# Expanding probabilities by masked products in a recurrent-memory attention kernel, with the output halves exchanged and the instruction order written anew

## The chip, the cores and the metric

The kernel runs on one core of a Trainium2 chip. The metric is the device time of one execution in microseconds, median of several runs. One more execution is recorded by the hardware profiler; its durations are what the text works with.

## The reference

Four blocks follow each other on a sequence of 2048 tokens of width 512: A, B, A, B, each with a residual sum and a layer norm in front.

```
# A: recurrent memory, 64 segments of 32 tokens, 8 memory rows, 32 heads of 128
for s in range(64):
    h = concat([mem, x[32*s : 32*s+32]])          # 40 rows
    q, k, v = h @ Wq, h @ Wk, h @ Wv              # 32 heads
    p = softmax(mask(q @ k.T * scale))            # tokens causal, memory rows see all
    o = (p @ v) @ Wo                              # 40 x 512
    mem = o[:8]                                   # the next segment's memory
    outs.append(o[8:])
# B: linear attention, 32 heads of 16
pq, pk = phi(q), phi(k)                           # phi(t) = where(t > 0, t + 1, exp(t)) + 1e-6
o = (pq @ (pk.T @ v)) / (pq @ sum(pk) + 1e-6) @ wo
```

The memory of segment s + 1 needs the finished output of segment s, so block A is a recurrence of 64 steps. The memory rows need only the memory queries; the outputs of the tokens feed nothing but the residual.

## The kernel before

**Tiling.** Every 128 x 128 weight block is used as four column tiles of 32, so that a matmul is issued four times, on the tiles (0, 32j). A step s handles one segment. Groups of four steps share 128 tokens (a "block" G with g = s mod 4). The last 8 tokens of each segment are handled together for the whole group ("left" rows).

**A step of block A** (`a_layer`, loop at L2446) issues, under names that the order table uses too:
- `kq0`, `kq1`, `v`: projections of the 40 rows by Wk, Wq, Wv (`project`, L2121 and, for matmuls that reuse loaded weights, L2010), each 512 columns wide, with copies out of PSUM by `evac` (L1893 on ScalarE, L1894 on VectorE, whichever the table names) and 32 x 32 transposes on VectorE (L2139).
- `mem0`, `mem1`: scores, softmax and weighted values of the 8 memory queries (`mem_attention`).
- `out`: 64 matmuls with Wo (`out_proj`, L2346). Their result lies in PSUM in two halves of 64 partitions that have to be added: one half is copied to `outW_sb` (`evac`), then the other half in PSUM and the copy are added into `y_sb` (L2355, on VectorE). An "urgent" output is that of a step; a non-urgent one is that of the left rows of a group.
- `next`: two sets of matmuls that turn the first 8 rows of y_sb round (L2372), and a copy into the input of the next step. `out` to `next` to `kq0` of step s + 1 is the recurrence.
- `res`: the output rows are moved by DMA into dx_sb, one on the POOL queue and one on SP's (L1909), and added to x (L2416).
- `x`: the attention of the 32 token queries (`x_attention`, L2262 on), whose result is used by `out` of step s + 1. The masked exponentials PQ (L2276) are summed (L2287), the reciprocal comes as exp(-ln) (L2290, L2292), the probabilities are normalised in place (L2294, and L2295 for the left keys). Then they are **expanded**: the partitions 32j to 32j + 31 hold the keys of head group j, and the matmuls need, for each j, a tile Pbx that is zero outside these partitions. Pbx is set to zero once, and each step makes four copies of 32 partitions x 256 elements, on ScalarE or VectorE. Pbl for the left keys is made by a masked product (L2301). The matmuls `pvx` (L2022) read Pbx, and their result is copied out.

**Block B** is interleaved. `b_in` handles 128 tokens: `layernorm` (L2058 to L2064), a transpose of the normalised rows by DMA from SP's queue (`turn`, L2049, kind "dtb"), projections (L2513), phi (L2486 to L2488) and sums. `prepare` normalises the next 128 tokens of block A and has them transposed in the same way (kind "dtx"), with five copies into the inputs of the steps. `b_out` has the queries transposed (kind "dtq").

**Order.** Nothing is scheduled on the chip: each engine runs its instructions in the order written, with semaphore waits. The order comes from the table PLACE, one entry for each (layer, step, name): a due time in ns for each operation in the order of its issue, with "a" (ScalarE) or "v" (VectorE) behind it where either engine could do it. `schedule` sorts all operations by these due times and gives out the eight PSUM banks in that order. The table was made by a planner that knew a cost for each operation; the numbers `cost` and `lat`, and the marks `quad` (start quadrant of what is read, and of what is written) are for that planner, and change nothing in the program itself.

Of the kernel before, what the change touches and what calls it, by code (L numbers as in the profile page):

```python
# [6 lines left out]
F32 = mybir.dt.float32  # L7
F32R = mybir.dt.float32r
ACTF = mybir.ActivationFunctionType
ALU = mybir.AluOpType  # L10
# [6 lines left out]
    (0, -9, 'setup'): '6123 501 3261 6844 6847 6850 7372 7373 7741 8707 11389 26847 27280 27283 30185 31770 36506 38205 39802 41695 45140 47037 6849 0 1070 1630 2700 3260 6121 6122 6124 6845 6846 6848 7371 7740 8300 10031 11387 11388 11536 12012 12013 12220 12780 13340 14071 14460 15020 15580 16140 36507 31771 16700 17260 17820 18373 27282a 7740 7966v 121034 26200 27281 29822 31769 33223 26849 27279 33872',  # L17
    (0, -4, 'start'): '8706v',
    (0, -2, 'left0'): '25336 25767 26846 27278 27918a 29821 30547v 31270',
    (0, -2, 'left1'): '29823 30186 30547 31271 32259a 32389 33224a 33509',  # L20
    (0, -2, 'leftv'): '35270 35702 36508 36665 37305a 37946 38425 38424a 39333 42302',
    (0, -2, 'prep'): '6120 6843 7037 7370 7742 8300 13340v 11386a 8533v 32390a 10032a',
    (0, -2, 'spin4'): '18429',
    (0, 0, 'kq0'): '24904 26415 27926 28573 29214v 32260 29214a 30184',
    (0, 0, 'kq1'): '14070 15020 15020 17260 26199 27918 28357 29005 18374v 26848 31270a 32752',
    (0, 0, 'mem0'): '31768 32752 35702 33509 36665 38092 40257 42302 43407 43810',
    (0, 0, 'mem1'): '34007 36133 36505 36665 36774 39801 39803 43409 44930 45625',
    (0, 0, 'next'): '48918 48972 49238v',
    (0, 0, 'out'): '44931 44932 45137 45347 46599 46818 47370 47588 48015a 48443',
    (0, 0, 'ql'): '31155v 33222v',  # L30
    (0, 0, 'v'): '40256 40258 41217 41219 42665v 41719a',
    (0, 0, 'x'): '37798 37954 38917 39332 39800 44674 43408a 40255v 40259a 40576v 44929 45138 47036 47095 48443 53855v 59925a 44674 44929 45566 46056 52710v 47038v',
    (0, 0, 'xl'): '500',
    (0, 1, 'kq0'): '50187 50188 50343 50775 52071v 53366 51639a 52502',
    (0, 1, 'kq1'): '51206 51638 51854 52285 51422 52070 52501 52717 52709a 53955 53856a 54093',
    (0, 1, 'mem0'): '53796 53854 54226 54819 54495 54876 55196 55952 55951 56442',
    (0, 1, 'mem1'): '54818 55196 55368 55953 55637 56114 56441 57401 56578 57403',
    (0, 1, 'next'): '59604 59658 59924v',
    (0, 1, 'out'): '56745 56964 57182 57400 57619 57839 58294 58295 58714a 59128',
    (0, 1, 'ql'): '50186v 37797a',  # L40
    (0, 1, 'res'): '66853 69592',
    (0, 1, 'v'): '52933 53365 53954 54496 55369v 55954a',
    (0, 1, 'x'): '56065 56440 57402 57619 57838 58853 58713v 58433v 58293v 58573v 59713 59414 59532 59770 59941 60357v 61029v 59355 59473 59712 59926 63405a 60150v',
    (0, 2, 'kq0'): '60165 60597 61028 61460 62756v 63619 63403a 63404',
    (0, 2, 'kq1'): '61892 62323 62539 62971 62107 62755 63187 63402 63677a 64680 63827v 64798',
    (0, 2, 'left0'): '32789 33221 38204 38917 40575a 41216 41694v 43407',
    (0, 2, 'left1'): '31826 32258 37097 41696 44067v 45136 45626a 47588',
    (0, 2, 'leftv'): '41218 45139 45624 46168 47588v 49345 49823 51206a 51206 51854',
    (0, 2, 'mem0'): '63618 64108 64679 64480 65161 65712 66473 66854 66845 67481',
    (0, 2, 'mem1'): '65503 65711 66204 66496 66472 66852 67171 67480 66963 67842',  # L50
    (0, 2, 'next'): '70334 70388 70654v',
    (0, 2, 'out'): '67694 67696 68577 69032 69033 69034 69593 69594 69595a 69962',
    (0, 2, 'prep'): '10030 10753 10947 11280 11535 12011 14073a 14074a 15580a 31272a 14072a',
    (0, 2, 'ql'): '56745v 60030v',
    (0, 2, 'res'): '70443 80542',
    (0, 2, 'v'): '63676 64208 64798 65071 65711a 66205v',
    (0, 2, 'x'): '66844 67480 67693 68108 68576 69591 69311v 69031v 69171v 69451v 70388 69726 69961 70442 70654 70973v 72191a 69785 69843 69902 70654 70972a 75960a',
    (0, 3, 'kq0'): '70972 71327 71758 72190 73054a 73919 73918v 73920',
    (0, 3, 'kq1'): '73053 73701 73917 74133 72622 72838 73323 73485 74839a 75762 74349a 75271',
    (0, 3, 'mem0'): '74348 75270 75642 75761 75961 76601 76711 77376 77376 77746',  # L60
    (0, 3, 'mem1'): '75370 75962 76602 76600 77208 77746 77869 78178 77746 78539',
    (0, 3, 'next'): '81000 81054 81319a',
    (0, 3, 'out'): '78178 78391 78807 79730 79731 80010 80012 80150 80425a 80543',
    (0, 3, 'ql'): '69731v 66907a',
    (0, 3, 'res'): '84592 87832',
    (0, 3, 'v'): '74407 74838 75428 75963 76600v 77209a',
    (0, 3, 'x'): '77415 77869 78390 78806 79274 79729 79869v 80009v 80149v 80149a 80288 80424 80541 80659 80888 84159v 84594a 80482 80600 80718 80776 81569v 82433v',
    (0, 4, 'kq0'): '81568 82000 82432 82863 84591a 85081 84160a 84595',
    (0, 4, 'kq1'): '83511 84374 84590 84806 83295 83727 83943 84158 85230a 85871 84806a 85302',
    (0, 4, 'mem0'): '85022 85302 86049 86048 86539 87288 87833 88902 88736 89139',  # L70
    (0, 4, 'mem1'): '86480 86538 87289 87288 88051 88268 88588 89252 89546 89885',
    (0, 4, 'next'): '92400 92454 93084a',
    (0, 4, 'out'): '90143 90483 90484 90485 90486 90963 90964 91625 91723a 92212',
    (0, 4, 'ql'): '80011a 79869a',
    (0, 4, 'res'): '95561 95991 85080 85871 86638 87831 88050 88518 88899 89140 89545v 90482 95345 91624 95985 95986 93833 90966 91626 92284 96274',
    (0, 4, 'v'): '85871 86048 86856 87400 88381a 88900v',
    (0, 4, 'x'): '87288 88380 89139 89465 90142 91624 91721a 90822v 90965a 91722v 91628 92152 92211 92270 93562 95344v 102252a 93563 93564 96854 98366 100384v 103118a',
    (0, 4, 'xl'): '2130',
    (0, 5, 'kq0'): '93565 93566 93832 94264 95562a 95984 95560v 95992',
    (0, 5, 'kq1'): '94695 94911 95127 95559 95343 95987 95990 96274 95983a 98481 96630a 97935',  # L80
    (0, 5, 'mem0'): '96913 96971 98366 97934 98480 98574 99186 99789 99791 99950',
    (0, 5, 'mem1'): '98477 98946 99066 99788 99790 99792 100073 100382 99950 101014',
    (0, 5, 'next'): '103383 103437 103702a',
    (0, 5, 'out'): '100383 101011 101012 101479 101480 101934 102074 102075 102427v 102777',
    (0, 5, 'ql'): '86050a 90962v',
    (0, 5, 'res'): '111729 109466',
    (0, 5, 'v'): '96630 97452 97502 97934 99187v 98574a',
    (0, 5, 'x'): '99793 100382 100594 101010 101478 101933 102073v 102637v 102425a 102076a 103480 103702 103703 103726 104819 106011a 107306v 103491 103702 103785 103844 105795v 107522v',
    (0, 6, 'bi'): '96914 97452 98367 98479 98482 98946 98478 102426 103119 109837 111575 112302 112818 115257 116071v 122296 125666 125780 128352 114679 115050 116913 129770',
    (0, 6, 'kq0'): '103956 104387 104931 105362 106658v 107730 106013a 107953',  # L90
    (0, 6, 'kq1'): '106657 106873 107089 107305 105794 106010 106226 106441 107729a 108975 107523a 108443',
    (0, 6, 'left0'): '55370 55519 58853 59128 62755v 73324 73701a 75960',
    (0, 6, 'left1'): '66204 66474 69596 81108 81747a 84593 86638a 88901',
    (0, 6, 'leftv'): '76603 80151 91627 91720 92454v 93083 93567 93561a 103117 106014',
    (0, 6, 'mem0'): '108384 108442 108976 109614 109465 110224 110916 110955 110357 111317',
    (0, 6, 'mem1'): '109405 109464 110223 109836 110600 110804 111727 111730 110915 111981',
    (0, 6, 'next'): '114624 114678 114944v',
    (0, 6, 'out'): '111726 111981 112162 112381 112599 112817 113036 113254 113714a 114142',
    (0, 6, 'prep'): '18373 24904 38092 41220 45755 53954 55368v 73322a 62971a 67695v 82000v',
    (0, 6, 'ql'): '101013v 104931v',  # L100
# [1672 lines left out]
def _build_kernel(nc, A_x, A_mem0, A_Wq, A_Wk, A_Wv, A_Wo, A_seg_len, B_wqkv, B_wo, out):  # L1773
# [274 lines left out]
    def turn(o, i, reads, writes, kind, lat=2.8):  # L2048
        add("sp", lambda e: e.dma_start_transpose(o, i), 1.2, reads=reads, writes=writes, dsem=kind, lat=lat)  # L2049
# [673 lines left out]
```

## Time and profile before

| | |
|---|---|
| median of 3 runs | 1614.55 us (1612.61 to 1621.16) |
| profiled execution | 1630.0 us |
| its span, first to last instruction | 1627.4 us |
| granted TensorE clock | 0.998 |
| TensorE busy | 1534.2 us (94%) |
| VectorE busy | 1226.8 us (75%) |
| ScalarE busy | 1059.4 us (65%) |
| GpSimd busy | 191.6 us (12%) |
| quadrant copies on ScalarE | 228, 94.3 us |
| quadrant copies on VectorE | 284, 62.2 us |

PE is TensorE's matmul row, PEld its weight loads, DVE is VectorE, ACT is ScalarE, POOL is GpSimd and SP is SyncE, which issues DMAs only. A line such as "PE pb L2372 <- DVE y_sb L2355" says that PE, at line 2372, sat idle until VectorE's instruction of line 2355 was done. A busy share is an average over the span. PE's ends are modelled, so that a busy PE need not be at its peak.

### The profile page before, as it was taken

How to read it: one execution, taken by the hardware profiler on the slowest of the kernel's cores; microseconds unless marked ns; L12 is line 12 of the kernel's file. 1: busy time of each engine (PE TensorE's matmuls, PEld its weight loads, DVE VectorE, ACT ScalarE, POOL GpSimd, SP SyncE). 2: the span in 40 equal slices, each digit the busy share in tenths (PEclk: the TensorE clock that was granted, in tenths of full speed). 3: DMA queues.
4: the chain of work that ended last, by engine and by line, in shares of the span. 5: the costliest groups of instructions: out<-in, count | busy, mean ns of one | idle time of the engine just before them, and what ended most of it. 6: DMA issues, size and time to landing. Idle time of an engine off the chain costs nothing.

```text
span 1627.4 us, 97760 instructions
## 1 busy us (share of the span) xinstructions
PE 1534.2 (94%) x48853; PEld 810.1 (50%) x40499; DVE 1226.8 (75%) x3601; ACT 1059.4 (65%) x3099; POOL 191.6 (12%) x388
## 2 busy tenths in 40 slices
PE   5889999999999999999899999999999999999997
PEld 1445555455555555555444555455555445555453
DVE  3778778877777877777678777777777777777777
ACT  2566666666666667666466677766677667676665
POOL 2011110111111011111101110111110111110110
PEclk9999999999999999999999999999999999999999
DMA  9310000110000001001101101111001110100115
GB/s 382 88 32 23 20 13 22 19 27 20 23 20 14 22 23 23 20 16 24 22 14 19 26 14 25 27 26 23 21 19 23 26 25 19 27 17 21 27 33 145
DMA packets 79348, 58.14 MB, mean 36 GB/s; under 512 B 58872, under 2 KB 73624, under 8 KB 77400
## 3 DMA queue, kind: packets, MB, share of 16 engines
q1 hardware_dynamic: 65912, 36.30, 8.5%
q0 software_dynamic: 12864, 15.46, 3.4%
q8 instruction: 350, 5.73, 1.5%
q14 instruction: 62, 0.51, 0.1%
q10 hardware_dynamic: 160, 0.14, 0.0%
HBM read 25.57 MB, written 10.35 MB: 22 GB/s over the span
## 4 chain that ended last, share of the span: by engine, by line
PE 68%; DVE 13%; DMA 10%; ACT 7%; issue 2%; POOL 0%; SPq 0%; DVEq 0%
PE pb L2121 25%; PE pb L2010 17%; PE pb L2346 12%; PE pb L2022 8%; DMA arena_sb<-arena_sb 5%; DVE arena_sb L1894 3%; ACT arena_sb L1893 2%; DMA dx_sb<-y_sb 2%; DMA Wv_sb<-in_A_Wv_dram 2%; DVE arena_sb L2139 2%; PE pb L2513 2%; PE pb L2210 1%; DVE y_sb L2355 1%; DVE arena_sb L2294 1%; PE pb L2372 1%
## 5 line engine op out<-in xcount | busy, mean ns | idle before, releaser
L1893 ACT ACTIVATE arena_sb<-pb 128x512 bf16<-128x512 f32 (+4 forms) x1032 | 499.6, 511 | 293.1 <-PE pb L2010 131.5
L1894 DVE CAST arena_sb<-pb 128x512 bf16<-128x512 f32 (+3 forms) x614 | 322.3, 533 | 105.7 <-PE pb L2010 64.9
L2121 PE MATMUL pb<-Wk_sb,arena_sb 128*32 128x512 bf16 x4096 | 363.3, 381 | 8.2 <-DMA Wk_sb<-in_A_Wk_dram 4.3
L2346 PE MATMUL pb<-Wo_sb,arena_sb 128*32 128x256 bf16 x10368 | 340.0, 273 | 5.7 <-issue 3.3
L2139 DVE STREAM_TRANSPOSE arena_sb<-arena_sb 128x256 f32<-128x256 f32 x640 | 263.3, 431 | 55.0 <-ACT arena_sb L1893 49.0
L2346 PEld LDWEIGHTS pb<-Wo_sb,arena_sb 128*32 128x32 bf16 x10368 | 257.7, 96 | 53.5 <-issue 15.9
L2022 PE MATMUL pb<-arena_sb 128*32 128x128 bf16 (+2 forms) x10800 | 266.6, 209 | 18.3 <-DVE arena_sb L1894 10.0
L2121 PE MATMUL pb<-Wq_sb,arena_sb 128*32 128x512 bf16 x3072 | 266.9, 379 | 3.3 <-DVE arena_sb L1894 2.8
L1909 POOL DMA_DIRECT2D dx_sb<-y_sb x252 | 128.4, 513 | 1198.5 <-DVE y_sb L2355 776.5
L2022 PEld LDWEIGHTS pb<-arena_sb 128*32 128x32 bf16 x10800 | 183.5, 96 | 149.5 <-DVE arena_sb L1894 45.5
L2121 PE MATMUL pb<-Wv_sb,arena_sb 128*32 128x512 bf16 x2560 | 251.4, 378 | 2.3 <-ACT arena_sb L1893 1.2
L2010 PE MATMUL pb<-Wv_sb,arena_sb 128*32 128x512 bf16 x2560 | 251.2, 378 | 0.0
L2121 PEld LDWEIGHTS pb<-Wk_sb,arena_sb 128*32 128x32 bf16 x4096 | 110.5, 97 | 196.4 <-issue 97.3
L2010 PE MATMUL pb<-Wq_sb,arena_sb 128*32 128x512 bf16 x2048 | 200.7, 379 | 0.0
L1893 ACT ACTIVATE arena_sb<-arena_sb 32x256 bf16<-32x256 bf16 (+2 forms) x411 | 146.9, 361 | 38.8 <-DVE arena_sb L2294 29.1
L2121 PEld LDWEIGHTS pb<-Wq_sb,arena_sb 128*32 128x32 bf16 x3072 | 83.8, 96 | 93.6 <-issue 43.6
L1894 DVE COPY arena_sb<-arena_sb 32x256 bf16<-32x256 bf16 (+2 forms) x502 | 100.8, 203 | 20.6 <-DMA arena_sb<-arena_sb 11.3
L2355 DVE TENSOR_TENSOR y_sb<-pb,outW_sb 64x256 bf16<-64x256 f32 x162 | 67.8, 419 | 55.4 <-ACT outW_sb L1893 51.3
L2258 DVE TENSOR_TENSOR arena_sb<-pb,arena_sb 128x128 bf16<-128x128 f32 x252 | 73.1, 290 | 47.3 <-PE pb L2022 15.2
L2121 PEld LDWEIGHTS pb<-Wv_sb,arena_sb 128*32 128x32 bf16 x2560 | 70.1, 95 | 66.1 <-issue 36.9
L2010 PE MATMUL pb<-Wk_sb,arena_sb 128*32 128x512 bf16 x1024 | 101.6, 379 | 0.0
L1893 ACT ACTIVATE outW_sb<-pb 64x256 f32<-64x256 f32 x130 | 49.0, 377 | 73.5 <-PE pb L2346 71.3
(110 smaller groups left out, 1793.2 us busy)
## 6 DMA issues: line engine op xcount, KB each, us to landing
Wk_sb<-in_A_Wk_dram SPq DMA_DIRECT2D x1, 4096.0 KB, 13.7
Wq_sb<-in_A_Wq_dram SPq DMA_DIRECT2D x1, 4096.0 KB, 24.1
Wv_sb<-in_A_Wv_dram SPq DMA_DIRECT2D x1, 4096.0 KB, 33.5
Wo_sb<-in_A_Wo_dram SPq DMA_DIRECT2D x16, 256.0 KB, 7.3
xs_scratch<-x_sb POOLq DMA_DIRECT2D x32, 128.0 KB, 2.2
pq_scratch<-arena_sb POOLq DMA_DIRECT2D x31, 128.0 KB, 2.4
x_sb<-xs_scratch POOLq DMA_DIRECT2D x16, 128.0 KB, 3.0
dx_sb<-y_sb SPq DMA_DIRECT2D x126, 12.0 KB
```

The source lines that it names most:

```text
L1893: return e.activation(o() if callable(o) else o, i() if callable(i) else i, ACTF.Copy)
L1894: return e.tensor_copy(o() if callable(o) else o, i() if callable(i) else i)
L1909: add(eng, lambda e: e.dma_start(o, i), 0.55 if eng == "pool" else 0.66, reads=reads, writes=writes, dsem="%s%d" % (kind, k), lat=lat + (0 ...
L2010: return pe.add_instruction(mybir.InstMatmult(name=nc.get_next_instruction_name(), engine=mybir.EngineType.PE, ins=[pe.lower_ap(x), pe.low ...
L2022: r = pe.matmul(o[q], w[:, q], x, start=start, stop=stop, skip_group_check=True, tile_position=(0, 32 * j))
L2121: r = pe.matmul(o, blk[:, c, :], w, start=(c == 0), stop=(c == 3), tile_position=(0, 32 * j))
L2139: add("dve", lambda v: v.transpose(dst, src(img[:, k, :].bitcast(F32))), 0.445, reads=[("img", k)], writes=[dkey])
L2210: r = pe.matmul(o, kT[:, hh, j // 2, :, j % 2], qT[:, hh, j // 2, :, j % 2].rearrange("p (k x) -> p k x", k=5), start=True, stop=True, til ...
L2258: add("dve", lambda v: v.tensor_tensor(oTb[:, s % NO, 16 * b:16 * b + 16, 0:8].rearrange("p (i j) q -> p j i q", i=4), heads(pv.f32()[:, 0 ...
L2346: r = pe.matmul(tl.f32()[32 * j:32 * j + 32, 0:256], oT[:, 4 * hh + n, :], Wo_sb[:, 8 * n + hh, 256 * d:256 * d + 256], start=(hh == 0 and ...
L2355: add("dve", lambda e: e.tensor_tensor(y_sb[0:64, k, :], tl.f32()[a, 0:256], outW[c, v, :], ALU.add), c_dve(256), reads=[("outW", w)], til ...
L2513: r = pe.matmul(dst.f32()[q, :], xlnT[:, c, q], wqkv_sb[:, c, o:o + D], start=c == 0, stop=c == 3, skip_group_check=True, tile_position=(0 ...
```

## The change

1. The four copies into quadrants of Pbx become two VectorE products, one for each half b of the heads, of the normalised probabilities with the block mask `bo_sb` (ones where the partition belongs to group j). Each product writes all 128 partitions, zeros included, so that Pbx need not be set to zero beforehand. The `pvx` matmuls of a half wait for that half's product alone.
2. In `out_proj` the two halves change places: for urgent outputs partitions 0 to 63 are copied and 64 to 127 read by the sum in PSUM, for non-urgent ones the other way round. `quad` tells the planner.
3. `turn` has a longer `lat` (3.6, and 4.4 for kind "dtb", in place of 2.8), and PLACE is written anew throughout, 1509 entries, with other due times and other choices of engine.

```diff
 PLACE = {
-    (0, -9, 'setup'): '6123 501 3261 6844 ...
+    (0, -9, 'setup'): '6124 561 6121 6125 ...
...
-    def turn(o, i, reads, writes, kind, lat=2.8):
-        add("sp", lambda e: e.dma_start_transpose(o, i), 1.2, reads=reads, writes=writes, dsem=kind, lat=lat)
+    def turn(o, i, reads, writes, kind, lat=3.6):
+        add("sp", lambda e: e.dma_start_transpose(o, i), 1.2, reads=reads, writes=writes, dsem=kind, lat=4.4 if kind == "dtb" else lat)
...
-            for j in range(4):
-                q = slice(32 * j, 32 * j + 32)
-                add(ANY, copy(Pbx[q, j, :, :], px[q]),
-                    {"act": c_act(256, 0, 1), "dve": c_dve(256, 4)}, quad=(j, j), reads=pk + [("Px", r2)], writes=[("Pbx", j)])
+            for b in range(2):
+                add("dve", lambda v, b=b: v.tensor_tensor(
+                    Pbx[:, :, b, :].rearrange("p j (k x) -> p j k x", k=4),
+                    px[:, b, :].rearrange("p (k x) -> p k x", k=4).unsqueeze(1).to_broadcast([128, 4, 4, 32]),
+                    bo_sb[:, :].rearrange("p (j x) -> p j x", j=4).unsqueeze(2).to_broadcast([128, 4, 4, 32]), ALU.mult),
+                    c_dve(512, 2), reads=pk + [("Px", r2), "bo"], writes=[("Pbx", b)])
...
-                        reads=[("Pbx", j) for j in range(4)] + [("v", r2, b)] + ([("vl", g2, b), "Pbl"] if i == 3 else []),
+                        reads=[("Pbx", b), ("v", r2, b)] + ([("vl", g2, b), "Pbl"] if i == 3 else []),
...
-            a, c = (slice(0, 64), slice(64, 128))[::1 if urgent else -1]
+            a, c = (slice(0, 64), slice(64, 128))[::-1 if urgent else 1]
             v = w if urgent else 0
-            evac(outW[c, v, :], lambda: tl.f32()[c, 0:256], 256, tiles=[tl], writes=[("outW", w)])
+            nd = evac(outW[c, v, :], lambda: tl.f32()[c, 0:256], 256, tiles=[tl], writes=[("outW", w)])
+            nd.quad = (0, 0) if urgent else (2, 2)
             add("dve", lambda e: e.tensor_tensor(y_sb[0:64, k, :], tl.f32()[a, 0:256], outW[c, v, :], ALU.add),
-                c_dve(256), reads=[("outW", w)], tiles=[tl], writes=[("y", k)])
+                c_dve(256), reads=[("outW", w)], tiles=[tl], writes=[("y", k)], quad=(2, 0) if urgent else (2, 1))
...
-            add("dve", lambda v: v.memset(Pbx[:, :, :, :].rearrange("p j b x -> p (j b x)").bitcast(F32), 0.0), 0.7,
-                writes=[("Pbx", j) for j in range(4)])
```

## The prediction

> **What bounds the kernel now.** First the page: busy time by engine, and the chain that ended last.
>
> ```profile
> PE 1534.2 (94%) x48853; PEld 810.1 (50%) x40499; DVE 1226.8 (75%) x3601; ACT 1059.4 (65%) x3099; POOL 191.6 (12%) x388
> ...
> PE 68%; DVE 13%; DMA 10%; ACT 7%; issue 2%; POOL 0%; SPq 0%; DVEq 0%
> ```
>
> TensorE (PE) is the bound. The change leaves every matmul as it is, so it can only move PE's idle time: 1627.4 - 1534.2 = 93.2 us. Next, where that lies, by stretches of 100 us (PE busy is the first figure behind the comma): the first loses 21.6 us to loading, the middle ones 2 to 7 us each.
>
> ```profile
> 0.00:100.00 100.00, 78.39 (x2165) 34.70 (x1671) 57.84 (x166) 42.91 (x126) 14.96 (x50) 1.00 0.53 193
> ...
> 400.00:500.00 100.00, 97.83 (x3202) 52.48 (x2641) 79.28 (x241) 68.49 (x205) 11.44 (x22) 1.00 0.09 21
> ...
> 700.00:800.00 100.00, 92.68 (x3044) 51.66 (x2588) 73.19 (x214) 59.40 (x171) 14.42 (x28) 1.00 0.10 20
> ```
>
> Then what ended PE's idle time (us in total, times, longest):
>
> ```profile
> PE pb L2513 <- DMA arena_sb<-arena_sb: 14.4, 13, 1.9
> PE pb L2022 <- DVE arena_sb L1894: 10.0, 28, 1.3
> ...
> PE pb L2372 <- DVE y_sb L2355: 6.1, 20, 0.8
> ...
> PE pb L2022 <- ACT arena_sb L1893: 3.9, 12, 0.6
> ```
>
> The largest single cause is L2513, the projections of the linear block, waiting for the DMA transpose of the normalised rows (L2049). The other lines are the three further places that the change touches: L2022 waits, among others, for the quadrant copies of the probabilities, L2372 for the add of the output halves. Last, the transpose by itself, from issue to landing:
>
> ```profile
> DMA to landing us min/median/max: 2.4/3.0/5.2
> ```
>
> The planner's table had 2.8 us for it. In the trace it takes either about 2.45 us or 3.1 to 5.0 us, and the 13 waits fall on the long ones.
>
> **The change, part by part.** All against the profiled execution, 1630.0 us (span 1627.4 and 2.6 around it). The median of the runs shown, 1614.55, is 0.9905 of that.
>
> *Order for later transposes.* The order table holds due times; I use them for order and distance alone. In the 30 input blocks whose rows are transposed by DMA, the distance from the normalisation (L2064) to the first matmul that reads the transpose goes from 2.68 us at least, 3.52 in the median, to 3.86 and 5.01. In the trace the transpose issues 0.03 us behind the normalisation (0.38 in three cases), and after the change too nothing else of SP's queue is ordered between the two, so landing stands at 2.4 to 5.1 us. Nearly all 13 waits then fall away; for the rest I keep 2.0 us: -12.4. A PE that no longer waits there meets the next late input sooner; I give a quarter back (bounds: all, or nothing): **-9.3**. The transposes that feed the memory block delay copies off PE (DVE waits 11.3 us for them, ACT 3.4): **-1**, bounds -4 and 0.
>
> *Four copies become two products.* Rows by form, and one step's stretch of VectorE (DVE):
>
> ```profile
> L1894 DVE COPY arena_sb<-arena_sb 32x256 bf16<-32x256 bf16 x284 | 62.2, 219 | 8.2
> ...
> L2301 DVE TENSOR_TENSOR arena_sb<-arena_sb 128x256 bf16<-128x256 bf16 x128 | 36.1, 282 | 2.2
> ...
> L2416 DVE TENSOR_TENSOR x_sb<-x_sb,dx_sb 128x512 bf16<-128x512 bf16 x30 | 12.1, 405 | 7.1 <-DMA dx_sb<-y_sb 5.2 <-issue 1.8
> ...
> L1893 ACT ACTIVATE arena_sb<-arena_sb 32x256 bf16<-32x256 bf16 x228 | 94.3, 414 | 33.3 <-DVE arena_sb L2294 29.1
> ```
>
> ```profile
> 405.53 0.68 DVE L2488 SCALAR_TENSOR_TENSOR arena_sb<-pb,arena_sb 128x512 bf16<-128x512 f32 x1
> 406.13 0.41 DVE L2294 TENSOR_TENSOR arena_sb<-arena_sb 128x256 bf16<-128x256 bf16 x1
> 406.58 0.22 DVE L2295 TENSOR_TENSOR arena_sb<-arena_sb 128x64 bf16<-128x64 bf16 x1
> 406.83 0.72 DVE L1894 COPY arena_sb<-arena_sb 32x256 bf16<-32x256 bf16 x3
> 407.59 0.29 DVE L2301 TENSOR_TENSOR arena_sb<-arena_sb 128x256 bf16<-128x256 bf16 x1
> ```
>
> Removed: 284 copies on DVE (62.2 us) and 228 on ScalarE (ACT, 94.3 us). Added: 256 products of 128x512 bf16, priced by L2416, the same shape and types without broadcast, at 405 ns; L2301 has such broadcast operands at half the size and keeps to the same line (282). That is 103.7 us: by durations DVE gains 41.5 us and ACT loses 94.3. By starts it is less. In the stretch an operation on all 128 partitions starts 0.08 us before its predecessor ends (405.53 + 0.68 = 406.21, next start 406.13), while each copy on a quadrant waits for the end and 0.03 more, as the operation behind it does (406.83 + 0.72 = 407.55, next 407.59). So a step's 2.2 copies hold DVE for 2.2 x 0.25 + 0.11 = 0.67 us, and two products for 2 x 0.325 = 0.65: nothing. The Trainium skill, "VectorE: DVE Perf Modes", section "Two Vector instructions with no wait between them", has the rule: an instruction whose input or output starts in another quadrant than the last one's is held until all earlier ones have finished. The trace agrees (0.03 us behind against 0.08 before).
>
> The table also moves casts from DVE to ACT: net 26 of 512 columns (685 ns), 13 of 384 (545), 14 small copies (186), 10 of next_mem (190), 4 output halves (424) and 2 others, less 8 of 128 (276) and 10 of 96 (176) that come back: 27.5 us. So by durations DVE +14.0 us to 1241 (76%), ACT about -69 to 990 (61%). Where DVE is not later, that is hidden under PE; if the cover goes, the 14.0 us are the price.
>
> For PE: of the 13.9 us that L2022 waits for L1894, 6.3 are for the quadrant copies (the single waits in the trace). The first half's products now start after one operation, not four, and the order takes them 0.6 us earlier (median distance from normalised probabilities 2.3 to 1.6 us). **-1**, bounds -6.3 and +6.3. The memset that goes lies under loading: 0.
>
> *Halves change places.* The urgent half is now copied on partitions 0 to 63, the sum reads PSUM at 64 to 127. The 32 non-urgent outputs of before have just that orientation: ACT copy (23 of them) 358 to 378 ns against 378, and no 0.03 us behind the predecessor but about 0.1 before its end; add 426 against 416. In 126 steps that is +1.3 us and about as much back where ACT ran right up to the copy (under half of the steps, 0.12 us each, about 5 us, of which half reaches PE). **-2**, bounds -5 and +1.3.
>
> *The rest of the order* changes everywhere and can't be priced singly: 0, and for the range the spread of the undisturbed 100 us stretches, 2.2 to 6 us idle around 4, over some 14 stretches: ±28 at the utmost.
>
> Sum: -9.3 - 1 - 1 - 2 = -13.3; 1630.0 - 13.3 = 1616.7; times 0.9905 = **1601.4 us**, 0.8% less. About 0.5% (8.1 us: below 1606.5, above 1622.6) is what a measurement of this kernel can tell from no change.
>
> **Rivals.**
> *The waits only move* (0.23). PE no longer waits for transposes, but for the evacuations and the recurrence behind them, 1630 - 13.3 + 13 or so: about 1614. For: PE's idle time has some thirty other causes of 1 to 8 us. Against: the chain of waits runs through these transposes in pieces of 3.5 to 5.2 us, so PE had little else to do.
>
> *DVE in front of the recurrence* (0.16, slower). All expansion now stands in DVE's queue, ahead of the add L2355 that PE awaits in 97 of 126 steps (48.3 us of weight loads waiting for it). Behind a pair just running the add is 0.37 us later on average: 97 x 0.37 = 36 us, 1630 - 13.3 + 36 = 1652.7, times 0.9905 = 1637. It makes the kernel slower from 22 us on, 0.23 us a step. For: DVE is at 79% in the middle, and the table's last due time is 14.2 us later, though with other latencies written in, so no measure. Against: only 33 of 130 adds have a product due in the 0.45 us before them, 31 had a copy there. The skill's same page, "The DRAIN you can't avoid", says that the next operation doesn't start until the pipe is empty. By that all 41.5 us added on DVE would count, (1630 - 13.3 + 41.5) x 0.9905 = 1642; the stretch above shows starts 0.08 us early, and so speaks against it.
>
> *The product isn't at the packed rate* (0.04). Then it takes as long as L2655, 676 to 684 ns with a 4-byte operand: 256 x 0.275 = 70 us more on DVE, half of it on the path: 1637. Against: L2301 and L2233 (279 ns) have the same broadcasts and the packed rate.
>
> **How the numbers follow.** Forecast 0.57, waits move 0.23, slower 0.16 + 0.04. The forecast's own range is 1588 to 1606.5; its low end takes all gains at their bounds (-30 us: 1585). 80% range: 1586 to 1630; left out are some 0.06 below, and 0.14 above, most of the two slow cases. Faster 0.57, same 0.23, slower 0.20.
>
> **What would show it.** L2513's wait for the DMA falls from 14.4 to under 4 us; the landing stays at 2.4 to 5.2. The product shows x256 at about 405 ns; DVE busy 1235 to 1245, ACT 985 to 1000. L2372's wait for L2355 doesn't grow beyond 6.1 and the weight loads' not beyond 48. PE busy stays at 1534 within a few us and the span falls to about 1614. Wrong if the DMA's wait goes and the span doesn't fall (the first rival), or if L2355 is awaited longer (the second).

## The result, and the profile after

The changed kernel takes 1598.5 us (median of 4 runs), the kernel before 1614.9. The ratio of their means is 0.9889, 95% interval 0.9854 to 0.9925. Run again with the experiments it came to 0.989 (0.9867 to 0.9912), some 18 us. The forecast was 1601.4. The profiled execution fell from 1630.0 to 1601.1 us, more than the median, because the one recorded before was the longest of its kernel's runs.

Busy time and the chain that ended last, on the page of the changed kernel:

```profile
PE 1526.6 (95%) x48853; PEld 825.0 (52%) x40499; DVE 1222.2 (76%) x3519; ACT 975.2 (61%) x2924; POOL 191.5 (12%) x388
...
PE 80%; DVE 6%; DMA 6%; ACT 5%; issue 2%; POOL 0%; SPq 0%; DVEq 0%; ACTq 0%; POOLq 0%
```

PE's idle time falls from 93.2 to 72.7 us, and its busy time by 7.6 us, though the matmuls are the same. The chain runs through PE for 80% of the span, where it was 68%, and DVE's part falls from 13% to 6%, though DVE has as much to do as before.

Part of these differences belongs to the long execution that was recorded before. The nearest trace of the old order at an ordinary length is that of the kernel before with the output halves exchanged and nothing else (`b_halves` below; 1619.8 us, its median 1619.5):

```profile
PE 1530.6 (95%) x48853; PEld 809.5 (50%) x40499; DVE 1223.0 (76%) x3601; ACT 1054.8 (65%) x3099; POOL 191.6 (12%) x388
...
PE 69%; DVE 13%; DMA 8%; ACT 7%; issue 2%; SPq 0%; DVEq 0%
```

```profile
PE pb L2513 <- DMA arena_sb<-arena_sb: 7.4, 8, 1.8
```

Its span is 1616.2 us, so PE is idle for 85.6 us there, and it waits 7.4 us for the transposes, not 14.4. The chain has nearly the shares of the kernel before. What ended PE's idle time in the changed kernel (us in total, times, longest):

```profile
PE pb L2375 <- DVE y_sb L2358: 5.2, 14, 0.8
...
PE pb L2022 <- DVE arena_sb L1894: 3.5, 11, 0.4
...
PE pb L2022 <- ACT arena_sb L1893: 0.8, 2, 0.6
...
PE pb L2514 <- DMA arena_sb<-arena_sb: 0.7, 1, 0.7
```

The wait for the transposes (now at L2514) is 0.7 us, with the landing as wide as ever:

```profile
DMA to landing us min/median/max: 2.4/2.7/5.7
```

Three more views follow: the product by form, the add of the halves from its tile's rows (ns: least, median, most), and a step's stretch of DVE (start and duration in us).

```profile
L2298 DVE TENSOR_TENSOR arena_sb<-arena_sb,bo_sb 128x512 bf16<-128x512 bf16 x256 | 102.5, 416 | 2.3
```

```profile
L2358 DVE TENSOR_TENSOR y_sb<-pb,outW_sb x162: 416/426/427, 48.8 to 1563.1; 64x256 bf16<-64x256 f32 x162
```

```profile
402.92 0.42 DVE L2294 TENSOR_TENSOR arena_sb<-arena_sb 128x256 bf16<-128x256 bf16 x1
403.38 0.42 DVE L2298 TENSOR_TENSOR arena_sb<-arena_sb,bo_sb 128x512 bf16<-128x512 bf16 x1
403.72 0.22 DVE L2295 TENSOR_TENSOR arena_sb<-arena_sb 128x64 bf16<-128x64 bf16 x1
403.86 0.42 DVE L2298 TENSOR_TENSOR arena_sb<-arena_sb,bo_sb 128x512 bf16<-128x512 bf16 x1
404.19 0.28 DVE L2303 TENSOR_TENSOR arena_sb<-arena_sb 128x256 bf16<-128x256 bf16 x1
```

A product holds DVE for 0.34 us (403.38 to 403.72) and 0.33 us (403.86 to 404.19): each successor starts 0.08 us or more before the product ends. In the prediction's sum by durations DVE was to gain 14 us; its busy time, which counts an overlap once, falls by 4.6.

### The profile page after: what moved, and what is told of

Its sections match the earlier page's. It is cut to its first block, busy times and chain, and to the rows that moved or that the text cites. A ratio compares the mean times of both kernels' runs of the same rounds, so it can differ in the third digit from the quotient of the medians.

```text
span 1599.3 us, 97508 instructions
## 1 busy us (share of the span) xinstructions
PE 1526.6 (95%) x48853; PEld 825.0 (52%) x40499; DVE 1222.2 (76%) x3519; ACT 975.2 (61%) x2924; POOL 191.5 (12%) x388
## 4 chain that ended last, share of the span: by engine, by line
PE 80%; DVE 6%; DMA 6%; ACT 5%; issue 2%; POOL 0%; SPq 0%; DVEq 0%; ACTq 0%; POOLq 0%
PE pb L2121 29%; PE pb L2010 21%; PE pb L2348 17%; PE pb L2022 8%; DMA dx_sb<-y_sb 2%; DMA Wv_sb<-in_A_Wv_dram 2%; ACT arena_sb L1893 2%; PE pb L2514 2%; PE pb L2210 1%; DVE arena_sb L1894 1%; PE pb L2287 1%; DVE y_sb L2358 1%; PE pb L2375 1%; DMA arena_sb<-arena_sb 1%; ACT outW_sb L1893 1%
## 5 line engine op out<-in xcount | busy, mean ns | idle before, releaser
L1893 ACT ACTIVATE arena_sb<-pb 128x512 bf16<-128x512 f32 (+4 forms) x1070 | 517.1, 512 | 343.8 <-PE pb L2010 194.4
L1894 DVE CAST arena_sb<-pb 128x512 bf16<-128x512 f32 (+3 forms) x574 | 298.4, 528 | 83.0 <-PE pb L2010 53.5
L2348 PEld LDWEIGHTS pb<-Wo_sb,arena_sb 128*32 128x32 bf16 x10368 | 260.7, 97 | 52.7 <-DVE arena_sb L2258 14.7
L2022 PE MATMUL pb<-arena_sb 128*32 128x128 bf16 (+2 forms) x10800 | 272.1, 208 | 8.0 <-DVE arena_sb L1894 3.1
L2022 PEld LDWEIGHTS pb<-arena_sb 128*32 128x32 bf16 x10800 | 191.8, 96 | 133.3 <-issue 28.6
L1893 ACT ACTIVATE outW_sb<-pb 64x256 f32<-64x256 f32 x134 | 50.7, 378 | 106.7 <-PE pb L2348 87.0
L2298 DVE TENSOR_TENSOR arena_sb<-arena_sb,bo_sb 128x512 bf16<-128x512 bf16 x256 | 102.5, 416 | 2.3
L2229 ACT ACTIVATE arena_sb<-pb 128x160 bf16<-128x160 f32 x256 | 77.6, 307 | 16.7 <-PE pb L2210 11.3
```

Source lines behind the costliest of these rows:

```text
L1893: return e.activation(o() if callable(o) else o, i() if callable(i) else i, ACTF.Copy)
L1894: return e.tensor_copy(o() if callable(o) else o, i() if callable(i) else i)
L2022: r = pe.matmul(o[q], w[:, q], x, start=start, stop=stop, skip_group_check=True, tile_position=(0, 32 * j))
L2229: add("act", lambda a: a.activation(PQ[:, r2, b, 64:224], tl.f32()[:, 64:224], ACTF.Exp, scale=SCALE), c_act(160), tiles=[tl], writes=[("P ...
L2298: add("dve", lambda v, b=b: v.tensor_tensor(Pbx[:, :, b, :].rearrange("p j (k x) -> p j k x", k=4), px[:, b, :].rearrange("p (k x) -> p k ...
L2348: r = pe.matmul(tl.f32()[32 * j:32 * j + 32, 0:256], oT[:, 4 * hh + n, :], Wo_sb[:, 8 * n + hh, 256 * d:256 * d + 256], start=(hh == 0 and ...
```

## The experiments

All ratios are to the kernel before, run on the same chip in turn; 0.001 is 1.6 us. The runs lie on three chips, so that two ratios are often compared across chips; the changed kernel's is 0.989 (0.9867 to 0.9912). A *hold* is what the prediction's stretch of DVE shows at the quadrant copies: an instruction starts some 0.03 us behind its predecessor's end instead of before it.

Three theories are set against each other. **W**: the waits for the transposes are the larger part of the gain. **L**: the load of VectorE and ScalarE and the holds at changes of quadrant are. **O**: only the order as a whole counts.

### Moving the distance by hand

The kernel before with the readers of the transpose later (`_late`, 0.1 to 2.0 us) and the normalisation earlier (`_early`, up to 1.2 us), block by block as the order allowed:

```diff
+        _v[0:6] = [(_t - _early, _e) for _t, _e in _v[0:6]]
+        _v[7:] = [(_t + _late, _e) for _t, _e in _v[7:]]
```

> The kernel before with one thing done: in 30 input blocks the matmuls that read the DMA transpose (and what follows them) get a later place, or the normalisation an earlier one, so that the distance between them is about 5.0 us instead of 3.5 (three are left at 3.3 to 3.7). Theory W (the waits for the transposes are the larger part of the gain): PE's wait at L2513 falls from 14.4 to under 4 us and the time by 7 to 11 us, ratio 0.993 to 0.996. Theory L (the load and the holds of VectorE and ScalarE are the larger part) and theory O (only the order as a whole counts): the wait goes, the time moves by less than 4 us, ratio 0.998 to 1.002.

Measured: 1.0342 (1.0321 to 1.0362), 55 us slower. The changed kernel with the normalisation later:

```diff
+        _last = min(_t for _t, _e in _v[7:11]) - 1
+        _v[0:6] = [(min(_t + (1400 if _k[:2] == (0, 18) else 1500), _last), _e) for _t, _e in _v[0:6]]
```

> The changed kernel with one thing undone: in the same blocks the normalisation stands 1.5 us later, so that the distance to the matmuls that read its transpose is about 3.5 us again. Theory W: PE's wait for the DMA comes back to 8 to 15 us and the time rises by 6 to 11 us, ratio to the kernel before 0.993 to 0.996. Theories L and O: the wait comes back, the time rises by less than 3 us, ratio 0.988 to 0.991.

Measured: 1.0098 (1.0073 to 1.0123), some 34 us above the changed kernel. And the kernel before with all three edits:

> The kernel before, in its own order, with all three edits: the longer distance to the transposes, two products in the places of the first two copies, the halves exchanged. It lacks only the rest of the new order. Theory W: ratio 0.991 to 0.995, nearly all from the distance. Theory L: 0.988 to 0.993, and more than half of it not from the distance. Theory O: 0.995 to 1.002, since the order was not made for the new operations.

Measured: 1.0338 (1.0318 to 1.0359). Beside them the changed kernel ran again, for comparison:

> The changed kernel once more, beside the other three on one chip, to narrow its interval: 0.987 to 0.991 of the kernel before by every theory.

Measured: 0.989 (0.9867 to 0.9912).

No theory had the times of the three. PE's waits in the first:

```profile
PE pb L2379 <- DVE y_sb L2362: 23.3, 41, 1.3
...
PE pb L2520 <- DMA arena_sb<-arena_sb: 2.2, 4, 0.6
```

and in the second:

```profile
PE pb L2519 <- DMA arena_sb<-arena_sb: 19.4, 14, 2.5
PE pb L2027 <- DVE arena_sb L2238: 10.4, 20, 1.4
```

The wait for the transpose went as all theories said, and came back larger than they said (19.4 us, where 8 to 15 were expected). But the add of the halves is now awaited for 23.3 us instead of 6.1 in the first, and the memory probabilities (L2238) for 10.4 instead of 4.2 in the second. A likely reason, not tested by itself, is that what was moved along (phi and its copies in the first, the normalisation in the second) now stands in its engine's queue in front of that work. So moving instructions doesn't price this wait. The third, beside the first, says that products and halves change next to nothing on top (0.0004).

### Taking the dependence away instead

Nothing is moved; the projections of 30 input blocks read weights in place of the transposed rows:

```diff
+        held = xlnT if end else wqkv_sb
...
-                                r = pe.matmul(dst.f32()[q, :], xlnT[:, c, q], wqkv_sb[:, c, o:o + D], ...
+                                r = pe.matmul(dst.f32()[q, :], held[:, c, q], wqkv_sb[:, c, o:o + D], ...
...
-                add("pe", mm, c_pe(len(parts), 512), reads=["wqkv", "xlnT"], tiles=[p[1] for p in parts])
+                add("pe", mm, c_pe(len(parts), 512), reads=["wqkv"] + ["xlnT"] * end, tiles=[p[1] for p in parts])
```

> The kernel before, order untouched, but the projections of the input blocks (L2513, 30 of 32 blocks) read a constant tile in place of the transposed rows; the transposes are still issued, and nobody waits for them. This leaves the dependence on the transpose out of the computation. It gives what the waits for the transposes are worth in the order of before, with nothing moved. Theory W (larger part of the gain): L2513's wait for the DMA is gone and the time is 8 to 13 us less, ratio 0.992 to 0.995. Theories L and O: less than 4 us, ratio 0.9975 to 1.001.

Measured: 0.9922 (0.9909 to 0.9934), 12.6 us less. In the changed kernel:

> The same in the changed kernel, where PE waits 0.7 us for these transposes. All theories: within 2 us of the changed kernel, ratio to the kernel before 0.987 to 0.990.

Measured: 0.9872 (0.9852 to 0.9892), 2.9 us below the changed kernel, within the intervals. In the order of before, then, the waits for the transposes are worth 12.6 us; in the new order nothing clear is left of them. For the order of before theory W's forecast holds. The chain of the first of the two, though, looks as before:

```profile
PE 70%; DVE 14%; ACT 7%; DMA 6%; issue 2%; SPq 0%; DVEq 0%
```

PE has 70% of it and DVE 14%, not the changed kernel's 80 and 6. Something else has changed in the changed kernel.

### Products and copies, each in the other's order

The kernel before with two products at the due times of the first two copies (the new product lines as in the change's diff):

```diff
+        _d = sorted(_t for _t, _e in _v[6:10])
+        _v[6:8] = [(_d[0], None), (_d[1], None)]
```

> The kernel before, in its own order, with two masked products in the places of the first two of the four copies, and nothing else. Theory W: within 3 us, since the copies cost PE 6.3 us at most and the products hold VectorE as long as the copies did, ratio 0.997 to 1.002. Theory L (load and holds of the two engines): 6 to 12 us less, ratio 0.9925 to 0.996, with ScalarE's busy time about 95 us lower. Theory O: 0 to 10 us more, for the order was not made for it.

Measured: 0.9991 (0.9981 to 1.0002), 1.5 us less. Its page and two of PE's waits:

```profile
PE 1534.7 (95%) x48853; PEld 821.6 (51%) x40499; DVE 1245.9 (77%) x3572; ACT 960.3 (59%) x2871; POOL 192.3 (12%) x388
```

```profile
PE pb L2380 <- DVE y_sb L2363: 8.4, 26, 0.8
PE pb L2354 <- issue: 8.2, 18, 0.9
```

ScalarE is 99 us lighter, DVE 19 us heavier, and the time stands still: theory L's 6 to 12 us are not there. The changed kernel with the four copies back, the zeroing of Pbx too, and the `pvx` matmuls waiting for all four:

```diff
+        _t = min(_v[6][0], _v[7][0])
+        _v[6:8] = [(_t, "act"), (_t, "dve"), (_t, "act"), (_t, "dve")]
```

> The changed kernel, in its own order, with the four quadrant copies back (two on ScalarE, two on VectorE, at the place of the earlier product), and nothing else undone. Theory W: 1 to 4 us slower than the changed kernel, ratio to the kernel before 0.989 to 0.992. Theory L: 6 to 12 us slower, ratio 0.993 to 0.997, with ScalarE's busy time about 100 us higher. Theory O: 5 to 20 us slower, as in the other direction.

Measured: 1.0162 (1.0147 to 1.0176), 44 us above the changed kernel, more than any theory had:

```profile
PE pb L2029 <- ACT arena_sb L1900: 18.4, 37, 1.3
```

PE waits 18.4 us at L2029 for ScalarE's copies out of PSUM and into Pbx, 0.8 in the changed kernel. By the single waits in the trace about 15 of them are for the quadrant copies. So this order leaves ScalarE little room for them at the place that they were given here; other places were not tried.

### The halves

Only the line of `a, c` is exchanged, in the kernel before and, backwards, in the changed one:

```diff
-            a, c = (slice(0, 64), slice(64, 128))[::1 if urgent else -1]
+            a, c = (slice(0, 64), slice(64, 128))[::-1 if urgent else 1]
```

> The kernel before, order untouched, with the output halves exchanged and nothing else. By the prediction's term 2 us less (between 5 less and 1.3 more), ratio 0.997 to 1.001; VectorE starts behind the add before its end in most steps, where before it waited. If the exchange is what the rest of the gain (5 us) comes from: ratio 0.996 to 0.998.

> The changed kernel with the output halves put back and nothing else. By the prediction's term 2 us slower than the changed kernel, ratio to the kernel before 0.989 to 0.992. If the exchange is what the rest of the gain comes from: 0.992 to 0.994.

Measured: 0.9985 (0.9971 to 0.9999), 2.4 us less, and 0.9896 (0.9877 to 0.9915), 1 us above the changed kernel and not to be told from it. In the traces of the kernel before and of the first run, the successor of the add was held behind it 90 times before and 42 times after the exchange, and started before its end 25 and 73 times (of 162).

### The holds alone

All four copies on partitions 0 to 31, same sizes, engines and order:

```diff
-                add(ANY, copy(Pbx[q, j, :, :], px[q]),
+                add(ANY, copy(Pbx[0:32, j, :, :], px[0:32]),
```

> The kernel before, order untouched, with all four copies of a step on partitions 0 to 31 (the other partitions' copies are left out of the computation, so that the products of all groups but the first are missing): same number, size and engines, but no change of quadrant. It gives the cost of the holds alone. If the holds cost only what the two engines can spare: less than 3 us, ratio 0.998 to 1.001, though the pairs of instructions held for 0.02 to 0.04 us fall by about half on both engines. If they are on PE's path: 5 to 12 us less, 0.9925 to 0.997.

Measured: 0.9851 (0.9827 to 0.9876), 24 us less, twice the most that was expected: as fast as the changed kernel, in the order of before. Its page and DVE's stretch in a step:

```profile
PE 1523.7 (95%) x48853; PEld 811.6 (51%) x40499; DVE 1200.0 (75%) x3601; ACT 1036.6 (65%) x3099; POOL 191.8 (12%) x388
...
PE 79%; DMA 8%; DVE 7%; ACT 3%; issue 1%; SPq 0%; POOL 0%; DVEq 0%
```

```profile
397.86 0.48 DVE L1894 COPY arena_sb<-arena_sb 32x256 bf16<-32x256 bf16 x3
398.26 0.27 DVE L2301 TENSOR_TENSOR arena_sb<-arena_sb 128x256 bf16<-128x256 bf16 x1
```

Three copies take 0.40 us from the first start to the successor's (397.86 to 398.26), where they took 0.76 before (406.83 to 407.59). The pairs of neighbours whose second starts 15 to 45 ns behind the first's end fall from 698 to 453 on ScalarE and from 902 to 559 on DVE (in the changed kernel they are 337 and 537). PE's waits at the same places:

```profile
PE pb L2513 <- DMA arena_sb<-arena_sb: 8.8, 10, 1.6
...
PE pb L2022 <- DVE arena_sb L1894: 5.8, 14, 1.2
...
PE pb L2372 <- DVE y_sb L2355: 3.5, 9, 0.8
```

They were 14.4, 10.0 and 6.1 us in the recorded execution of the kernel before, and 7.4, 9.8 and 6.8 with the halves exchanged. So the first did not fall for this reason; the other two did. Against that second trace PE's idle time is 10.7 us less (74.9) and its busy time 6.9. The granted clock doesn't explain it (0.999, and 1.0 there), and the 128 x 128 matmuls that read Pbx among others take 219 ns in both. The chain has the changed kernel's look, 79% PE. The holds are on PE's path, not in the engines' slack. The copies by themselves are a little shorter too, 208 for 219 ns and 406 for 414: 5 us of busy time, which this run doesn't separate from the holds.

The count of held pairs is no price by itself, though. With the products in the old order (the run above at 0.9991) it falls to 409 on ScalarE and 599 on DVE, about as far as here, and the time stands still.

### All but the rest of the order

The order of before with the constant tile, the products and the halves:

> The order of before with everything but the new order: input blocks' projections on a constant tile (no wait for the transposes, which leaves that dependence out of the computation), two products in the places of the first two copies, the halves exchanged. Beside the changed kernel on a constant tile (0.9872) it tells what the rest of the new order is worth. If the parts add up and the rest of the order is worth nothing: 0.987 to 0.989. If the rest of the order brings some 4 us: 0.989 to 0.992.

Measured: 0.9938 (0.9919 to 0.9956), 10 us less, a smaller gain than either case had. The parts alone had 12.6, 1.5 and 2.4: they don't add up. Beside the changed kernel on the constant tile (0.9872) it lacks only the rest of the new order, which is therefore worth 0.0066 or 10.7 us, give or take 4.4 (both intervals' halves, added as squares). PE's largest waits here, and the chain:

```profile
PE pb L2354 <- issue: 9.0, 19, 1.1
PE pb L2380 <- DVE y_sb L2363: 8.0, 25, 0.8
```

```profile
PE 74%; DVE 13%; DMA 5%; ACT 5%; issue 3%; SPq 0%; POOL 0%; DVEq 0%
```

The add of the halves is awaited longer than in either kernel, and DVE keeps 13% of the chain. With the products it falls to 6% only in the new order. Which of the new order's moves bring the 10.7 us, no run tells.

Of the theories, then, W holds for the order of before. L fails for the products as they are, which bring 1.5 us there, although the holds alone are worth up to 24. O has a part only: the rest of the order brings about as much as the transposes.

## Why the prediction was right, and where its terms were off

*Direction and size.* 1601.4 forecast, 1598.5 measured; 13.2 us less against 16 to 18 (12 to 24 by the interval).

*What the change can move.* The first step of the prediction was that only PE's idle time can move, since the matmuls stay. That holds in part: for the same 48853 matmuls PE's busy time was 1526.6 us in place of 1534.2, and between 1523.7 and 1549.9 in the other runs. So the idle time doesn't hold all that a change can bring; why the busy time varies is not shown.

*Transposes, -9.3.* Right in mechanism: the wait fell to 0.7 us, and in the order of before its removal alone brings 12.6 us (10.7 to 14.7). Whether a quarter is given back to "the next late input" can't be told. The 14.4 us came from one long execution; in the trace with only the halves exchanged, the same order otherwise, the wait was 7.4. Taken from 14.4, a gain of 12.6 gives an eighth back; taken from 7.4, it is more than the wait itself. That the term came out near the measured size is partly luck. The further -1 for the transposes that feed the memory block was not priced by a run; the copies' waits for them fell from 11.3 us on DVE and 3.4 on ScalarE to 0.8 and none.

*Copies to products, -1.* The net holds in the order of before: -1.5 (-3.1 to +0.3). The 13.9 us that the prediction gives to L1894 are those of L1894 and L1893 together (10.0 and 3.9), and so are the 6.3 us for the quadrant copies. The reasoning, that copies and products hold DVE alike (0.67 and 0.65 us a step), holds as well, in starts. What it missed is that these amounts are on PE's path. Copies without holds bring 24 us. The products remove the holds too, but put on DVE what ScalarE did: DVE's busy time is 1245.9 us against 1200.0 there, and some 22 of the 24 us are gone. That DVE's added work takes them back is read from these two pages; no run tried it by itself, and the place of the products in the old order may be as much to blame.

*Halves, -2.* Measured -2.4 (-4.7 to -0.2) in the order of before, and 1 us in the new one, which can't be told from none. The add took 426 ns as forecast; the copy took 378 and not less, so that the gain lies in the starts.

*The rest of the order, 0.* The term that was mis-sized: -10.7 ± 4.4 us, measured between two kernels without the wait for the transposes. Its bound of ±28 held it.

*The sum.* The right total rests on errors that cancel, and that is luck. The parts came to 16.5 us alone and to 10 together, so that terms added one by one promise too much, and the new order then made up for it.

*The signs.* The waits, the landing and the product came about as listed. Busy times did not: DVE 1222.2 us where 1235 to 1245 were forecast, ScalarE 975.2 where 985 to 1000 were, and PE as said above. The span fell to 1599.3 and not only to 1614, since the 1627.4 that the forecast started from were long.

*Rivals.* "The waits only move" fails: the wait went and the time fell. "DVE in front of the recurrence" fails for the changed kernel: the weight loads' wait for the add fell from 48.3 to 40.0 us. Its line before and after:

```profile
PEld pb L2372 <- DVE y_sb L2355: 48.3, 97, 1.0
```

```profile
PEld pb L2375 <- DVE y_sb L2358: 40.0, 81, 1.0
```

In the order of before the mechanism is seen in small, though, PE awaiting the add 8.4 us with the products in place of 6.1. That all 41.5 us added on DVE count fails as well: the successors of the products start 0.08 us before their end. What the prediction quotes there goes on in the same section of the Trainium skill ("VectorE: DVE Perf Modes", "The DRAIN you can't avoid"): an operation that is not held starts earlier. "Not at the packed rate" fails: 416 ns, 11 more than forecast.

*Why the parts don't add up* is open. PE's idle time at L2354 (the `out` matmuls) under "issue" has no releaser in the profile. It is 8 to 9 us in the two kernels with products in the old order and nothing moved, 4.7 where the transposes' readers were moved too, 3.3 in the kernel before and 3.7 in the changed kernel.

## What to carry to other kernels

To price a wait in a kernel whose order is written out, take away the dependence (other data) and not the place: moving the reader or the writer by up to 2 us cost 34 to 55 us here. An engine at 75% busy in a recurrence can still be on the path, through small pauses at every step: look at the pairs of instructions that don't overlap, not at the busy share alone, and price them by a run, since a like fall in their number brought 24 us in one kernel and 1.5 in another. Replacing many short operations by fewer long ones on the fuller engine may pay only with the order made anew: here the edit brought 1.5 us in the old order, and the rest of the new order about 10.7. And take the profile near the median: the wait of 14.4 us in a long execution was 7.4 in an ordinary one.

## What the runs showed of the hardware

- A change of start partition between neighbours costs an overlap. On DVE the successor starts about 0.08 us before the end without such a change and 0.03 behind it with one; on ScalarE about 0.10 before and 0.02 behind. The same copies, all on partitions 0 to 31, started about 0.07 and 0.09 us before their predecessor's end. Some 500 such copies, with all their neighbours, cost this kernel up to 24 us.
- The Trainium skill, "VectorE: DVE Perf Modes", section "Two Vector instructions with no wait between them", states the rule for VectorE: an instruction that starts in another quadrant than the last one is held until every earlier one has finished. The traces agree (902 held pairs on DVE, 559 with all four copies on partitions 0 to 31).
- A DMA transpose of 128 x 512 bf16 for the 30 input blocks landed at most 2.6 us after its issue in 14 cases of the kernel before, and after 3.3 to 5.0 in the other 16. In the changed kernel 17 landed by 2.6 and the last after 5.7. No run tells what decides.
- A masked product of 128 x 512 bf16 with two broadcast operands took 416 ns, the same shape without broadcast 405 to 415.
